# An attention and feed-forward kernel on one core: the activation h·erf(softplus(h)) as Softplus, Erf and one product, in place of Exp, Ln, a Newton step and Gelu

## The chip, the cores and the metric

The kernel runs on 1 core of one Trainium2 chip. The metric is device time in microseconds of one execution, as the median of several. One profiled execution of each kernel gives a trace; its span is from the first to the last instruction.

Engines in the profile: PE is TensorE's matmul, PEld its weight load, DVE is VectorE, ACT is ScalarE, POOL is GpSimd. The trace also gives the clock that TensorE was granted, as a share of full speed; below, "warm" is a stretch at 1.00 and "cold" one at 0.50, the two levels that single stretches show here.

## The reference, cut to what matters

```python
def _attn_ref(r, k, v, w, u):            # B, H, S, D = 4, 8, 768, 48
    for t in range(S):
        cur = einsum('bhd,bhe->bhde', u * kt, vt)
        y[:, :, t] = einsum('bhd,bhde->bhe', rt, state + cur)
        state = wt[..., None] * state + einsum('bhd,bhe->bhde', kt, vt)

def _moe_ref(x, w_in, w_out):            # x 3072 x 384, w_in 384 x 2048, w_out 2048 x 384
    h = x @ w_in
    sp = np.maximum(h, 0.0) + np.log1p(np.exp(-np.abs(h)))
    g = h * erf(sp)
    return g @ w_out
```

## The kernel before: the parts that matter

The attention works in 24 steps of 128 tokens; six steps (chunks) make one sequence. In a step, seven levels each do products `pp` of k and r on TensorE, then VectorE scales half of r and half of k in place (`in`), and the next level's products need them. Between the levels TensorE is given "fills": pieces of the feed-forward part, which works in units of two steps (256 tokens). TensorE's order is fixed by hand; the order on the other engines comes from a scheduler, and `in_turn` only keeps ScalarE's table passes in one sequence.

```python
for level in range(1, LOG + 1):
    ...                                   # pp = products of K and R (PE)
    fill(1)                               # one piece of feed-forward work (PE)
    for x, to, by in ((R, 1, 0), (K, 0, 1)):
        ...
        nc.vector.tensor_mul(half_of, half_of, tots[level - 1]...)        # "in"
    if level <= MASKED:
        nc.vector.copy_predicated(flat, mask..., pp...)                   # "a"
    else:
        ...  nc.scalar.copy(a[...], pp[...])
...                                       # y; transposes of K; the state's products
y_sb = ...; nc.scalar.copy(y_sb[:], y[:])
fill(1)
...                                       # transposes of y into xT

def hidden(xT, gs):                       # per group of 1024 columns; 4 groups to a unit
    in_turn(nc.scalar.preload_act_table_set("natural_log_exp_and_others"))
    ...                                   # h = x w_in (PE), copied by ACT
    nc.vector.tensor_scalar(out=ex[:], in0=h[:], scalar1=30.0, scalar2=None, op0=ALU.min)
    in_turn(nc.scalar.activation(ex[:], ex[:], AF.Exp, bias=e_bias[:]))
    in_turn(nc.scalar.activation(sp[:], ex[:], AF.Ln, bias=1.0, scale=1.0 / E_SCALE))
    in_turn(nc.scalar.activation(rc[:], sp[:], AF.Ln, bias=tiny[:]))
    in_turn(nc.scalar.activation(rc[:], rc[:], AF.Exp, scale=-1.0))
    nc.gpsimd.tensor_mul(er[:], sp[:], rc[:])
    nc.vector.scalar_tensor_tensor(out=rc[:], in0=er[:], scalar=2.0, in1=rc[:], ...)
    ...                                   # after the last group of the unit:
    in_turn(nc.scalar.activation(sp[:], sp[:], AF.Gelu, scale=math.sqrt(2.0)))

def gate(h, ex, sp, rc):
    nc.vector.scalar_tensor_tensor(out=low[:], in0=ex[:], ..., in1=ex[:], ...)
    nc.gpsimd.tensor_mul(rc[:], sp[:], rc[:])
    nc.vector.scalar_tensor_tensor(out=ex[:], in0=rc[:], ..., in1=ex[:], ...)
    nc.vector.scalar_tensor_tensor(out=ex[:], in0=low[:], ..., in1=ex[:], ...)
    nc.gpsimd.tensor_mul(h[:], ex[:], h[:])
```

The weights come as 64-bit numbers and are converted to fp32 at the start, by seven VectorE and two GpSimd passes per tile (24 tiles of w_in, 16 of w_out).

Of the kernel before, what the change touches and what calls it, by code (L numbers as in the profile page):

```python
# [17 lines left out]
P = 128  # partitions, and the tokens of one chunk  # L18
EP = 64  # partitions from one head of a pair to the other
UNIT = 256  # tokens of one feed-forward unit  # L20
GC = 1024  # columns of one group of the activation

# The decays between two tokens s < t of one chunk are split where the blocks of
# 2, 4, .. 128 tokens that hold both have their middle: at its level each pair
# gets (product of w from the middle up to t-1) x (product of w from s+1 up to
# the middle), so only products of w appear, never a quotient or a logarithm.
LOG = 7
MASKED = 5  # levels 1 .. MASKED are picked out of a full product by a mask


def rows(ap, n):
    """ap's last axis in rows of n"""
    return ap.rearrange("p (a b) -> p a b", b=n)
# [3 lines left out]
def kernel(  # L37
    ctx: ExitStack,
    tc: tile.TileContext,
    rkw: bass.AP,  # [step, e, d, (r k w), pair, t]  # L40
    v: bass.AP,  # [token, (h d)]
    u: bass.AP,  # [e, d, pair]
    w_in: bass.AP,
    w_out: bass.AP,
    masks: bass.AP,  # [s, level, t]
# [20 lines left out]
    act = ctx.enter_context(tc.tile_pool(name="act", bufs=NT // FG))  # L66
# [7 lines left out]
    # ---- what stays  # L74
# [8 lines left out]
    e_bias = const.tile([P, 1], FP32, name="e_bias")  # L83
    tiny = const.tile([P, 1], FP32, name="tiny")

    # The rows between the heads of a pair stay zero.
# [7 lines left out]
    E_SCALE = math.sqrt(2.0 / math.pi)  # L94
    LOW = math.sqrt(math.pi / 8.0)
    nc.vector.memset(e_bias[:], math.log(E_SCALE))
    nc.vector.memset(tiny[:], 1e-18)
# [11 lines left out]
    def load_weight(dst, src):  # L109
        """src into dst: fp32 as it is; fp64, of which the words come, rounded to fp32"""  # L110
        if src.dtype == FP32:
            nc.sync.dma_start(out=dst, in_=src)
            return
        n, f = dst.shape[1:]
        shape = [P, n, f]
        words = wide.tile([P, n, f, 2], I32, name="words")
        nc.sync.dma_start(
            out=words[:].rearrange("p n f two -> p n (f two)"), in_=src.bitcast(I32)
        )
        low, high = words[:, :, :, 0], words[:, :, :, 1]  # L120
        bits = wide.tile(shape, I32, name="bits")
        keep = wide.tile(shape, I32, name="keep")
        part = wide.tile(shape, FP32, name="part")
        SIGN, REST = -(1 << 31), (1 << 31) - 1
        # the exponent from 11 bits to 8, and the upper 20 bits of the mantissa
        nc.vector.tensor_scalar(
            out=bits[:], in0=high, scalar1=3, scalar2=1 << 30,
            op0=ALU.logical_shift_left, op1=ALU.bitwise_xor,
        )
        # what is below fp32's range is 0  # L130
        nc.vector.tensor_scalar(
            out=keep[:], in0=high, scalar1=REST, scalar2=None, op0=ALU.bitwise_and
        )
        nc.vector.tensor_scalar(
            out=keep[:], in0=keep[:], scalar1=float(0x382 << 20), scalar2=-1.0,
            op0=ALU.is_ge, op1=ALU.mult,
        )
        nc.vector.scalar_tensor_tensor(
            out=bits[:], in0=bits[:], scalar=REST, in1=keep[:],
            op0=ALU.bitwise_and, op1=ALU.bitwise_and,  # L140
        )
        nc.vector.scalar_tensor_tensor(
            out=bits[:], in0=high, scalar=SIGN, in1=bits[:],
            op0=ALU.bitwise_and, op1=ALU.bitwise_or,
        )
        # the lower 32 bits of the mantissa, by the power of two
        nc.vector.tensor_scalar(  # L147
            out=keep[:], in0=bits[:], scalar1=-(1 << 23), scalar2=None, op0=ALU.bitwise_and
        )
        nc.vector.tensor_scalar(  # L150
            out=part[:], in0=low.bitcast(U32), scalar1=2.0**-52, scalar2=None, op0=ALU.mult
        )
        nc.gpsimd.tensor_mul(part[:], part[:], keep[:].bitcast(FP32))  # L153
        nc.gpsimd.tensor_add(dst, part[:], bits[:].bitcast(FP32))
# [17 lines left out]
    def attend(s, xT, at, fill):  # L172
        """The tokens of step s, into the columns `at` of xT; fill(n) gives the tensor engine
        n pieces of other work."""
# [4 lines left out]
        # a[s, e, pair, t]: what v at s counts for in y at t  # L179
# [3 lines left out]
        def product(k, s0=0, t0=0, n=C, bank=None):  # L183
            """k of the n tokens from s0 on times R of those from t0 on"""
# [13 lines left out]
        # tots: the products of w over the blocks of 2**level tokens  # L198
# [11 lines left out]
        # A token with itself: through u.  # L210
# [9 lines left out]
        for level in range(1, LOG + 1):  # L220
# [8 lines left out]
            # R of the right halves by w of the left ones, K of the left by the right  # L229
# [20 lines left out]
        # y: from the chunks before, through the state, and from this one  # L250
# [23 lines left out]
        # the state behind this chunk, with zeros from head to head  # L274
# [36 lines left out]
    def in_turn(ins):  # L311
        """The activations in the order that switches tables least."""
        if last[0] is not None:
            tc.add_manual_dep(
                ins.ins,
                last[0].ins.name,
                mybir.DependencyInfo(mybir.DependencyClass.NoSync, mybir.DependencyReason.DATA),
                reason="activation tables",
            )
        last[0] = ins  # L320

    def hidden(xT, gs):
        """What gate() makes g / sqrt 2 of in h's place, g = h erf(sp), sp = log(1 + exp(h)),
        from gelu(z) = z (1 + erf(z / sqrt 2)) / 2 with z = sqrt(2) sp: erf(sp) / sqrt 2 =
        gelu(z) / sp - 1 / sqrt 2. Rounding would leave little of that far below h = 0: it is
        held between its bounds ex and ex - LOW ex^2, ex = sqrt(2 / pi) exp(h). Beyond h = 30
        erf(sp) is 1."""
        in_turn(nc.scalar.preload_act_table_set("natural_log_exp_and_others"))
        groups = []
        for g in range(NT // FG):  # L330
            h = hid.tile([P, FG, UNIT], FP32, name="h")
            for j in range(FG // 2):
# [14 lines left out]
            ex = act.tile([P, FG, UNIT], FP32, name="ex")  # L347
            sp = act.tile([P, FG, UNIT], FP32, name="sp")
            rc = act.tile([P, FG, UNIT], FP32, name="rc")
            nc.vector.tensor_scalar(  # L350
                out=ex[:], in0=h[:], scalar1=30.0, scalar2=None, op0=ALU.min
            )
            # ex = sqrt(2 / pi) exp(h)
            in_turn(nc.scalar.activation(ex[:], ex[:], AF.Exp, bias=e_bias[:]))  # L354
            in_turn(nc.scalar.activation(sp[:], ex[:], AF.Ln, bias=1.0, scale=1.0 / E_SCALE))  # L355
            # rc = 1 / sp, by a logarithm and a step of Newton
            in_turn(nc.scalar.activation(rc[:], sp[:], AF.Ln, bias=tiny[:]))  # L357
            in_turn(nc.scalar.activation(rc[:], rc[:], AF.Exp, scale=-1.0))  # L358
            er = act.tile([P, FG, UNIT], FP32, name="er", bufs=1)
            nc.gpsimd.tensor_mul(er[:], sp[:], rc[:])  # L360
            nc.vector.scalar_tensor_tensor(  # L361
                out=rc[:], in0=er[:], scalar=2.0, in1=rc[:],
                op0=ALU.subtract, op1=ALU.mult, reverse0=True,
            )
            groups.append((h, ex, sp, rc))
            if g == NT // FG - 1:
                for _, _, sp, _ in groups:
                    in_turn(nc.scalar.activation(sp[:], sp[:], AF.Gelu, scale=math.sqrt(2.0)))
                gs.extend(groups)
            yield  # L370

    def gate(h, ex, sp, rc):
        low = act.tile([P, FG, UNIT], FP32, name="low", bufs=1)
        nc.vector.scalar_tensor_tensor(  # L374
            out=low[:], in0=ex[:], scalar=-1.0 / LOW, in1=ex[:], op0=ALU.add, op1=ALU.mult
        )
        nc.gpsimd.tensor_mul(rc[:], sp[:], rc[:])  # L377
        nc.vector.scalar_tensor_tensor(  # L378
            out=ex[:], in0=rc[:], scalar=-math.sqrt(0.5), in1=ex[:], op0=ALU.add, op1=ALU.min
        )  # L380
        nc.vector.scalar_tensor_tensor(  # L381
            out=ex[:], in0=low[:], scalar=-LOW, in1=ex[:], op0=ALU.mult, op1=ALU.max
        )
        nc.gpsimd.tensor_mul(h[:], ex[:], h[:])  # L384

    def project(i, gs):
        """out of unit i"""
        for t in range(SPU):
# [12 lines left out]
            nc.scalar.mul(out=o[:], in_=ps[:], mul=math.sqrt(2.0))  # L401
# [3 lines left out]
    def pieces():  # L405
        """The feed-forward work in pieces of six or four products: half of a unit's hidden
        layer, half of the projection of the unit before, and again."""
# [47 lines left out]
def level_masks():  # L455
    """[s, level, t]: whether s and t meet at that level"""
# [45 lines left out]
```

## Time and profile before

| | before |
|---|---|
| median of 4 runs | 1239.9 us (1238.8 to 1246.9) |
| span of the profiled execution | 1249.1 us |
| start to step 2; step 2; step 3 | 114.3; 78.2; 53.0 us |
| steps 4 to 23 | 905.3 us |
| after the attention (tail) | 98.3 us |

The stages are read from the timeline of TensorE: each step begins with the products of `uk`. The page's first part gives each engine's busy time, with its share of the span and its instructions:

```profile
PE 959.8 (77%) x6232; PEld 725.6 (58%) x6232; DVE 877.3 (70%) x1040; ACT 413.3 (33%) x524; POOL 638.4 (51%) x438
```

### The profile page before, as it was taken

The page shows a single profiled execution, that of the slowest core. Times are in us where ns is not written, and L with a number is a line of the kernel's source. Part 1 is how long each engine was busy: PE and PEld are TensorE (multiplying, and loading weights), DVE is VectorE, ACT ScalarE, POOL GpSimd, SP SyncE. Part 2 cuts the span into 40 slices and gives each one's busy share as a digit, 9 for nine tenths or more (in the row PEclk, how much of TensorE's full clock was granted, in tenths as well). Part 3 has the DMA queues.
Part 4 walks back from the last instruction along what each step waited for, and adds up shares of the span by engine and source line. Part 5 has one row for each costly group of instructions (what it writes and reads, how often), then busy time and mean ns, then how long its engine had stood idle before and what let it go on. Part 6 is the DMA issues. An engine that isn't in the chain of part 4 may idle for free.

```text
span 1249.1 us, 15339 instructions
## 1 busy us (share of the span) xinstructions
PE 959.8 (77%) x6232; PEld 725.6 (58%) x6232; DVE 877.3 (70%) x1040; ACT 413.3 (33%) x524; POOL 638.4 (51%) x438
## 2 busy tenths in 40 slices
PE   3336528489699798798898898898898898898847
PEld 2336426467466666666666666666675675675624
DVE  6898884774875945946966936937957837838563
ACT  0001113333345136145135226225244324324440
POOL 5756562831933923923825725715627527516362
PEclk9999657599799689789798888888897887888978
DMA  5323211101100100100110110110010010000000
GB/s 137 93 80 107 73 53 26 26 1 33 32 19 15 32 20 13 32 20 13 33 32 1 33 33 1 32 33 18 15 33 20 14 33 7 1 7 7 7 6 13
DMA packets 16086, 37.49 MB, mean 30 GB/s; under 512 B 2320, under 2 KB 8464, under 8 KB 16016
## 3 DMA queue, kind: packets, MB, share of 16 engines
q1 hardware_dynamic: 16016, 36.51, 11.3%
q8 instruction: 49, 0.80, 0.3%
q14 instruction: 21, 0.17, 0.1%
HBM read 31.79 MB, written 4.72 MB: 29 GB/s over the span
## 4 chain that ended last, share of the span: by engine, by line
DVE 41%; PE 22%; ACT 13%; issue 11%; POOL 10%; DMA 1%; POOLq 0%; SPq 0%; DVEq 0%; ACTq 0%
DVE ex L378 8%; DVE in L234 7%; POOL er L360 7%; PE m L391 6%; PE m L337 6%; DVE low L374 6%; DVE ex L381 6%; PE pp L189 4%; ACT ex L354 3%; ACT rc L357 3%; ACT sp L355 3%; ACT rc L358 3%; DVE a L240 2%; DVE ex L350 2%; POOL part L153 2%
## 5 line engine op out<-in xcount | busy, mean ns | idle before, releaser
L391 PE MATMUL m<-w_out_sb,h 128*128 128x384 f32 x768 | 298.0, 538 | 25.4 <-POOL h L384 20.0
L360 POOL TENSOR_TENSOR er<-sp,rc 128x1024 f32<-128x1024 f32 x48 | 113.2, 2357 | 385.3 <-ACT rc L358 385.3
L189 PE MATMUL pp<-in 48*128 48x128 f32 (+2 forms) x3072 | 192.1, 275 | 144.3 <-DVE in L234 144.3
L337 PE MATMUL m<-xT,w_in_sb 128*128 128x256 f32 x1152 | 300.4, 416 | 0.6 <-ACT xT L307 0.6
L189 PEld LDWEIGHTS pp<-in 48*128 48x128 f32 (+2 forms) x3072 | 164.7, 181 | 199.8 <-issue 195.9
L337 PEld LDWEIGHTS m<-xT,w_in_sb 128*128 128x128 f32 x1152 | 231.4, 207 | 46.2 <-issue 3.1
L391 PEld LDWEIGHTS m<-w_out_sb,h 128*128 128x128 f32 x768 | 153.9, 210 | 125.8 <-POOL h L384 28.7
L234 DVE TENSOR_TENSOR in<-in,tot_sb 128x256 f32<-128x256 f32 x284 | 154.5, 579 | 47.5 <-PE pp L189 47.5
L361 DVE SCALAR_TENSOR_TENSOR rc<-er,rc 128x1024 f32<-128x1024 f32 x48 | 84.1, 1752 | 142.0 <-POOL er L360 142.0
L384 POOL TENSOR_TENSOR h<-ex,h 128x1024 f32<-128x1024 f32 x48 | 133.3, 2777 | 47.1 <-DVE ex L381 47.1
L344 ACT COPY h<-m 128x512 f32<-128x512 f32 x96 | 55.7, 580 | 306.4 <-PE m L337 306.4
L240 DVE COPY_PREDICATED a<-mask_sb,pp 128x1024 f32<-128x1024 int32 x120 | 155.9, 1299 | 0.0
L377 POOL TENSOR_TENSOR rc<-sp,rc 128x1024 f32<-128x1024 f32 x48 | 145.1, 3044 | 0.2
L378 DVE SCALAR_TENSOR_TENSOR ex<-rc,ex 128x1024 f32<-128x1024 f32 x48 | 103.5, 2156 | 6.8 <-POOL rc L377 3.9
L255 PE MATMUL y<-s,in 128*128 128x96 f32 x160 | 50.1, 409 | 66.3 <-DVE in L234 66.3
L374 DVE SCALAR_TENSOR_TENSOR low<-ex 128x1024 f32<-128x1024 f32 x48 | 95.2, 1983 | 2.3 <-ACT ex L354 1.2
L153 POOL TENSOR_TENSOR part<-part,keep 128x256 f32<-128x256 f32 (+1 forms) x40 | 61.6, 1540 | 56.9 <-DVE keep L147 56.9
L354 ACT ACTIVATE ex<-ex,e_bias 128x1024 f32<-128x1024 f32 x48 | 55.2, 1149 | 103.7 <-DVE ex L350 101.1
L207 POOL TENSOR_TENSOR tot_sb<-tot_sb 128x128 f32<-128x128 f32 (+5 forms) x140 | 79.9, 571 | 9.2
L265 PE MATMUL y<-v_sb,a 128*128 128x48 f32 x384 | 78.4, 349 | 6.5 <-ACT a L248 6.5
L255 PEld LDWEIGHTS y<-s,in 128*128 128x128 f32 x160 | 36.7, 282 | 77.3 <-DVE in L234 77.3
L265 PEld LDWEIGHTS y<-v_sb,a 128*128 128x128 f32 x384 | 76.7, 281 | 7.8 <-ACT a L248 7.0
(50 smaller groups left out, 943.9 us busy)
## 6 DMA issues: line engine op xcount, KB each, us to landing
in<-in_rkw SPq DMA_DIRECT2D x48, 288.0 KB, 4.6
words<-in_moe_w_in SPq DMA_DIRECT2D x24, 256.0 KB, 2.7
words<-in_moe_w_out SPq DMA_DIRECT2D x16, 384.0 KB, 3.1
v_sb<-in_v SPq DMA_DIRECT2D x24, 192.0 KB, 2.5
out<-o SPq DMA_DIRECT2D x24, 192.0 KB, 1.9
mask_sb<-in_masks SPq DMA_DIRECT2D x1, 320.0 KB, 3.4
u_sb<-in_u SPq DMA_DIRECT2D x2, 0.8 KB, 2.0
```

The lines of the kernel that those rows point to most:

```text
L189: nc.tensor.matmul(pp[s0 : s0 + n, e, p, t0 : t0 + n], lhsT=k[at_, p, s0 : s0 + n], rhs=R[at_, p, t0 : t0 + n], start=True, stop=True,)
L234: nc.vector.tensor_mul(half_of, half_of, tots[level - 1][:, :, by : by + 1].to_broadcast([P, nb, half]),)
L240: nc.vector.copy_predicated(flat, mask_sb[:, level - 1 : level, :].to_broadcast([P, NE * NP, C]), pp[:].rearrange("p e n t -> p (e n) t"),)
L265: nc.tensor.matmul(y[:, h], lhsT=a[:, e, p, :], rhs=vt[:, h], start=not c, stop=True, skip_group_check=True,)
L337: nc.tensor.matmul(ps[:, q, :], lhsT=w_in_sb[:, kk, f * P : (f + 1) * P], rhs=xT[:, kk, :], start=kk == 0, stop=kk == KT - 1,)
L354: in_turn(nc.scalar.activation(ex[:], ex[:], AF.Exp, bias=e_bias[:]))
L360: nc.gpsimd.tensor_mul(er[:], sp[:], rc[:])
L374: nc.vector.scalar_tensor_tensor(out=low[:], in0=ex[:], scalar=-1.0 / LOW, in1=ex[:], op0=ALU.add, op1=ALU.mult)
L377: nc.gpsimd.tensor_mul(rc[:], sp[:], rc[:])
L378: nc.vector.scalar_tensor_tensor(out=ex[:], in0=rc[:], scalar=-math.sqrt(0.5), in1=ex[:], op0=ALU.add, op1=ALU.min)
L384: nc.gpsimd.tensor_mul(h[:], ex[:], h[:])
L391: nc.tensor.matmul(ps[:], lhsT=gs[f // FG][0][:, f % FG, t * P : (t + 1) * P], rhs=w_out_sb[:, f, :], start=f == 0, stop=f == NT - 1,)
```

## The change

The intent: ScalarE has Softplus and Erf as functions of its own, so the activation needs two table passes and one product, and the roundabout through Exp, Ln, a Newton step, Gelu and a clamp goes. The diff, cut to its core (comments, which also went, left out):

```diff
-    act = ctx.enter_context(tc.tile_pool(name="act", bufs=NT // FG))
+    act = ctx.enter_context(tc.tile_pool(name="act", bufs=2 * NT // FG))
...
-        in_turn(nc.scalar.preload_act_table_set("natural_log_exp_and_others"))
+        in_turn(nc.scalar.preload_act_table_set("softplus"))
...
-            ...                     # min, Exp, Ln, Ln, Exp, er, rc as above
+            in_turn(nc.scalar.activation(sp[:], h[:], AF.Softplus))
...
-                    in_turn(nc.scalar.activation(sp[:], sp[:], AF.Gelu, scale=math.sqrt(2.0)))
+                    in_turn(nc.scalar.activation(sp[:], sp[:], AF.Erf))
...
-    def gate(h, ex, sp, rc):
-        ...                         # low, rc, ex, ex, h as above
+    def gate(h, sp):
+        nc.vector.tensor_mul(h[:], h[:], sp[:])
...
-            nc.scalar.mul(out=o[:], in_=ps[:], mul=math.sqrt(2.0))
+            nc.scalar.copy(o[:], ps[:])
```

More of the change, by code (lines that the diff above doesn't have):

```diff
@@ L1 @@
-import math
 from contextlib import ExitStack
@@ L82 @@
     w_out_sb = const.tile([P, NT, DM], FP32, name="w_out_sb")
-    e_bias = const.tile([P, 1], FP32, name="e_bias")
-    tiny = const.tile([P, 1], FP32, name="tiny")
     nc.vector.memset(in_bufs[0][:], 0.0)
@@ L93 @@
     make_identity(nc, ident[:])
-    E_SCALE = math.sqrt(2.0 / math.pi)
-    LOW = math.sqrt(math.pi / 8.0)
-    nc.vector.memset(e_bias[:], math.log(E_SCALE))
-    nc.vector.memset(tiny[:], 1e-18)
     loaded = {}
@@ L346, in hidden @@
                     yield
-            ex = act.tile([P, FG, UNIT], FP32, name="ex")
             sp = act.tile([P, FG, UNIT], FP32, name="sp")
-            rc = act.tile([P, FG, UNIT], FP32, name="rc")
-            nc.vector.tensor_scalar(
-                out=ex[:], in0=h[:], scalar1=30.0, scalar2=None, op0=ALU.min
-            )
-            in_turn(nc.scalar.activation(ex[:], ex[:], AF.Exp, bias=e_bias[:]))
-            in_turn(nc.scalar.activation(sp[:], ex[:], AF.Ln, bias=1.0, scale=1.0 / E_SCALE))
-            in_turn(nc.scalar.activation(rc[:], sp[:], AF.Ln, bias=tiny[:]))
-            in_turn(nc.scalar.activation(rc[:], rc[:], AF.Exp, scale=-1.0))
-            er = act.tile([P, FG, UNIT], FP32, name="er", bufs=1)
-            nc.gpsimd.tensor_mul(er[:], sp[:], rc[:])
-            nc.vector.scalar_tensor_tensor(
-                out=rc[:], in0=er[:], scalar=2.0, in1=rc[:],
-                op0=ALU.subtract, op1=ALU.mult, reverse0=True,
-            )
-            groups.append((h, ex, sp, rc))
+            in_turn(nc.scalar.activation(sp[:], h[:], AF.Softplus))
+            groups.append((h, sp))
             if g == NT // FG - 1:
-                for _, _, sp, _ in groups:
-                    in_turn(nc.scalar.activation(sp[:], sp[:], AF.Gelu, scale=math.sqrt(2.0)))
+                for _, sp in groups:
+                    in_turn(nc.scalar.activation(sp[:], sp[:], AF.Erf))
                 gs.extend(groups)
             yield
-    def gate(h, ex, sp, rc):
-        low = act.tile([P, FG, UNIT], FP32, name="low", bufs=1)
-        nc.vector.scalar_tensor_tensor(
-            out=low[:], in0=ex[:], scalar=-1.0 / LOW, in1=ex[:], op0=ALU.add, op1=ALU.mult
-        )
-        nc.gpsimd.tensor_mul(rc[:], sp[:], rc[:])
-        nc.vector.scalar_tensor_tensor(
-            out=ex[:], in0=rc[:], scalar=-math.sqrt(0.5), in1=ex[:], op0=ALU.add, op1=ALU.min
-        )
-        nc.vector.scalar_tensor_tensor(
-            out=ex[:], in0=low[:], scalar=-LOW, in1=ex[:], op0=ALU.mult, op1=ALU.max
-        )
-        nc.gpsimd.tensor_mul(h[:], ex[:], h[:])
+    def gate(h, sp):
+        nc.vector.tensor_mul(h[:], h[:], sp[:])
     def project(i, gs):
```

## The prediction

> **What bounds the kernel now.** I read the page's busy shares and chain first, then the list of waits, then the timeline of one step, and last the stretch table. On the page TensorE (PE) is busy 77% and VectorE (DVE) 70% of the span, so no engine is plainly full. The chain of work that ended last is mostly VectorE:
>
> ```profile
> DVE 41%; PE 22%; ACT 13%; issue 11%; POOL 10%; DMA 1%; POOLq 0%; SPq 0%; DVEq 0%; ACTq 0%
> ...
> L374 DVE SCALAR_TENSOR_TENSOR low<-ex 128x1024 f32<-128x1024 f32 x48 | 95.2, 1983 | 2.3 <-ACT ex L354 1.2
> ```
>
> The list of waits (total us, times, longest) says what TensorE is held up by:
>
> ```profile
> PE pp L189 <- DVE in L234: 144.3, 41, 11.3
> ...
> PE y L255 <- DVE in L234: 66.3, 20, 5.5
> ```
>
> Both are the same thing: the attention scales its r and k in place on VectorE (`in`) between two levels, and the next products wait. These scalings are short; what makes them late is seen in the timeline (start, us, engine, idle before) of the last part of one step:
>
> ```profile
> 757.72 1.16 PE L189 MATMUL pp<-in 48*128 48x128 f32 x16
> 758.81 2.85 PE L391 MATMUL m<-w_out_sb,h 128*128 128x384 f32 x8
> 761.59 0.60 PE L189 MATMUL pp<-in 48*32 48x32 f32 x32
> 762.12 2.85 PE L391 MATMUL m<-w_out_sb,h 128*128 128x384 f32 x8
> 764.90 0.68 PE L189 MATMUL pp<-in 48*64 48x64 f32 x16
> 765.51 2.85 PE L391 MATMUL m<-w_out_sb,h 128*128 128x384 f32 x8
> 767.66 5.64 POOL L377 TENSOR_TENSOR rc<-sp,rc 128x1024 f32<-128x1024 f32 x2
> 767.69 3.42 DVE L361 SCALAR_TENSOR_TENSOR rc<-er,rc 128x1024 f32<-128x1024 f32 x1 [4.53 <-POOL er L360]
> 771.03 2.89 DVE L234 TENSOR_TENSOR in<-in,tot_sb 128x256 f32<-128x256 f32 x2
> 773.64 0.74 PE L255 MATMUL y<-s,in 128*128 128x96 f32 x2 [5.28 <-DVE in L234]
> 774.18 0.98 PE L265 MATMUL y<-v_sb,a 128*128 128x48 f32 x4
> ```
>
> Up to 768.3 TensorE has no gap. Then `in` stands in VectorE's queue behind `rc` (L361), which had waited 4.53 us for GpSimd's (POOL's) `er`, and both then run against GpSimd: 2.89 us for two scalings that take 0.75 us elsewhere in the step. TensorE stands for 5.28 us and is slower afterwards. So the activation reaches the critical path through VectorE's queue, GpSimd's latency and contention between these two, not through TensorE's own work. The stretch table, from the start of step 4 to the end of the attention (length; then busy time and count of PE, PEld, DVE, ACT, POOL; clock), gives the size:
>
> ```profile
> 245.50:1150.80 905.30, 775.28 (x5189) 582.36 (x5188) 629.89 (x627) 344.00 (x437) 445.49 (x275) 0.87 0.08 20
> ```
>
> Twenty steps take 905.3 us, 45.3 each; TensorE idles 130 us of it (6.5 a step), at a clock of 0.87.
>
> **What the Trainium skill says.** (1) "ScalarE: Activation LUTs", What ACT_TABLE_LOAD costs: every function has the same per-element cost, and a switch of table costs the same for every set (1283 ns for the load). The trace agrees: Gelu 1045 ns and Ln, Exp 1057 ns (1149 ns with a bias tile), 24 loads of 1283 ns. So I give Softplus and Erf 1.05 us each. (2) "VectorE: DVE Perf Modes", The TRN2 errata: an fp32 tensor_tensor takes (N+151)/0.96 ns, 1.22 us for 1024; the trace's `a` (L214) took 1.223 us. (3) "GPSIMD Engine Reference", Specifications: GpSimd's SBUF interfaces are shared with VectorE, and two-input VectorE instructions contend. The trace agrees: L374 takes 1.199 us at its least, 3.265 at its most. (4) "TensorE: Matmul & The Clock Gate", Part 1: after an idle window of some 3.4 us the clock halves. The trace agrees: sixteen `pp` records take 1.16 us in a dense stretch and 2.08 us after the 4.12 us wait at 702.8.
>
> **The change part by part,** per group of 1024 columns (48 groups):
> - VectorE loses five passes: means of 802 + 1752 + 1983 + 2156 + 1644 ns = 8.34 us, 400 us in all. It gains one product of 1.22 us, 59 us. Its busy time goes from 877 to about 535 us, and to some 510 if the contention goes with it.
> - GpSimd loses `er`, `rc` and `h`: 2357 + 3044 + 2777 ns = 8.18 us, 392 us in all, and keeps about 247 us. Two hand-overs from VectorE to GpSimd and back vanish.
> - ScalarE loses five passes, 258 us by the rows, and gains two, 48 x 2 x 1.05 = 101 us: 413 to about 255 us. The number of table loads stays at 24 in the order of instructions. sqrt(2) in the output copy was free and stays so.
> - TensorE's instructions and their order do not change, nor does a byte from or to HBM.
>
> So the question is how short a step is when TensorE never waits. I add it up from warm stretches of the timeline. From `uk` at 741.31 to the last fill's end at 768.28 there is no gap: 26.97. The y products take 2.71 warm (730.38 to 733.09), the transposes of k with the wait for their copy 1.74, the state's products 1.81, the last fill 2.79 warm, and the transposes of y 0.42: **36.4 us**. The last chunk of a sequence has no state part (-3.55): 32.9 us. Of the 20 steps 4 are such, and 3 are a first chunk (about 1 us less each): 16 x 36.4 + 4 x 32.9 - 3 = 711 us, against 905: **-194 us**. Some 130 of this are waits; the rest is the clock.
>
> Does the rest of the new work fit under 36.4? VectorE has per step 14 scalings (5.3), five masked copies (6.5), 1.23 and 0.72 for `a` and the state, and two products on average (2.4): 16 us. ScalarE about 11 us. One place is tight: in the second step of each unit, softplus of the last group, the table load and four Erf follow the fourth fill, and the order of instructions has two products ahead of the level-6 scalings. From the fourth fill's end: copy to +0.7, softplus +1.75, load +3.1, Erf done at +4.1 and +5.0, products done at +6.5, scalings +7.25, which the next `pp` wants at +7.2. I allow 0.3 us a unit, 3 us in all.
>
> The first 114 us load and convert the weights, with no activation in them: unchanged. Step 2 (114.3 to 192.5) still converts 13 tiles of w_out. About 6 us of the activation's VectorE passes and its waits on GpSimd go: an estimate of 78 to 67. Step 3 (53.0) becomes a dense step with a cold start, 40. Together **-24**. The tail (1150.8 to 1249.1, 98.3 us) holds 24 pieces of fill at 2.79 = 67 us plus 3.5 us from the last product to the end; the last unit's softplus, load, Erf and product (8.4 us) lie under the last four pieces of the projection before it (11.1 us). So 70.5, **-28**.
>
> Sum: 1249.1 - 194 + 3 - 24 - 28 = 1006 us of profiled span. The timed median is 0.992 of it (1239.2 to 1249.1): 998. For waits that I do not see I add 1%: **1010 us**.
>
> **Rivals.** (a) *VectorE stays the limit of each level*, its queue held by the product that waits for Erf. For it: instructions are in order, and two products stand ahead of scalings. If each unit lost 3 us so, and the clock fell each time, 12 units would cost 40 to 60 us: 1050 to 1070. Against it: the sums above. (b) *ScalarE becomes the blocker*: the load and four Erf stand ahead of the copies of `a` that y needs. For it: y waited for them twice before, 6.5 us in all. Against it: the slack is about 1 us and ScalarE has less to do than before. A few us a unit: again about 1050. (c) *The gain is nearly nothing because the activation was hidden.* Then the waits for `in` would remain; but they begin behind the removed instructions in the timeline. I give it little. (d) The conversion in step 2 is bound by VectorE and GpSimd anyway and nothing is won there: +11 us.
>
> **Range and chances.** Without any new wait about 995, with (a) or (b) in every unit 1060; I take 980 to 1055. A gain under 2% would need nearly all waits to come back: faster 0.97, same 0.02, slower 0.01.
>
> **What would show it.** Right: TensorE busy above 90% between step 4 and the end of the attention at a clock near 1, steps of 36 to 38 us, waits for `in` under 30 us in total, VectorE near 520 us, GpSimd near 240, scalings at 0.41 us, a tail near 71 us. Wrong: TensorE still waiting for `in` with h<-h,sp just ahead of it (a), y waiting for the copy of `a` (b), Softplus costing more than 1.1 us, or step 2 still at 78 us (d).

## The result, and the profile after

The changed kernel takes 974.9 us in the median of 4 runs (973.4 to 980.0) and is correct. The ratio to the kernel before is 0.785, with a 95% interval of 0.781 to 0.789. A ratio here is not quite the ratio of the medians quoted. The prediction had the direction, the size within 4% and the mechanism, but 974.9 lies below its range of 980 to 1055: its pieces of TensorE work were sized too long, above all in the dense step.

| stage, us of span | before | predicted | after |
|---|---|---|---|
| start to step 2 | 114.3 | 114.3 | 112.6 |
| step 2 | 78.2 | 67 | 66.6 |
| step 3 | 53.0 | 40 | 37.4 |
| steps 4 to 23 | 905.3 | 714 | 688.3 |
| tail | 98.3 | 70.5 | 66.6 |
| sum | 1249.1 | 1006 | 971.6 |

The page of the changed kernel, busy times and the chain that ended last:

```profile
PE 852.1 (88%) x6232; PEld 649.6 (67%) x6232; DVE 485.2 (50%) x846; ACT 258.3 (27%) x380; POOL 191.1 (20%) x294
...
PE 80%; DVE 11%; POOL 3%; ACT 3%; issue 2%; DMA 1%; SPq 0%; POOLq 0%; ACTq 0%; DVEq 0%
```

The chain now runs through TensorE. TensorE itself is busy 108 us less with the same 6232 instructions, at a mean granted clock of 0.965 in place of 0.862. The waits of TensorE for the scalings (total us, times, longest):

```profile
PE pp L182 <- DVE in L227: 72.3, 19, 7.8
...
PE y L248 <- DVE in L227: 6.9, 3, 4.3
```

Of 210.6 us 79.2 are left, and they lie in the first four steps: between 250 and 900 us the list of waits has none of them. (Before, 92 of the 210.6 lay in the first four steps too.) The stretch table from step 4 to the end of the attention (length; busy time and count of PE, PEld, DVE, ACT, POOL; clock) shows TensorE standing 11.9 us of 688.3, at full clock:

```profile
216.67:905.00 688.33, 676.43 (x5189) 510.23 (x5188) 308.19 (x468) 214.08 (x316) 67.97 (x154) 1.00 0.11 26
```

So of the 217 us that these twenty steps lost, 118 were waits of TensorE (130 to 12) and 99 were the same products done at a higher clock (775.3 to 676.4, the clock from 0.87 to 1.00). In the tail TensorE had waited another 25.5 us for the last unit's own activation (20.0 for `h` of the gate, 5.5 for ScalarE's copy), which the list no longer has. The timeline of the end of a step, the place that the prediction showed with a stop of 5.28 us:

```profile
616.03 3.90 ACT L342 ACTIVATE sp<-sp 128x1024 f32<-128x1024 f32 x4
616.81 0.60 PE L182 MATMUL pp<-in 48*32 48x32 f32 x32
617.12 2.36 DVE L347 TENSOR_TENSOR h<-h,sp 128x1024 f32<-128x1024 f32 x2 [0.96 <-ACT sp L342]
617.34 2.85 PE L354 MATMUL m<-w_out_sb,h 128*128 128x384 f32 x8
619.39 0.76 DVE L227 TENSOR_TENSOR in<-in,tot_sb 128x256 f32<-128x256 f32 x2
620.07 2.35 DVE L347 TENSOR_TENSOR h<-h,sp 128x1024 f32<-128x1024 f32 x2
620.29 0.68 PE L182 MATMUL pp<-in 48*64 48x64 f32 x16
620.91 2.85 PE L354 MATMUL m<-w_out_sb,h 128*128 128x384 f32 x8
622.34 0.76 DVE L227 TENSOR_TENSOR in<-in,tot_sb 128x256 f32<-128x256 f32 x2
623.59 0.36 PE L248 MATMUL y<-s,in 128*128 128x96 f32 x2
```

Two products of the gate do stand in VectorE's queue ahead of the scalings, as the prediction's rival (a) has it, but each pair takes 2.36 us with GpSimd at rest, and y begins on time.

### The profile page after: what moved, and what is told of

Read it like the earlier page. It is cut to its first block, busy times and chain, and to the rows that moved or that the text cites. A ratio compares the mean times of both kernels' runs of the same rounds, so it can differ in the third digit from the quotient of the medians. Undisturbed runs are those within 1.5% of the kernel's fastest.

```text
span 971.6 us, 14797 instructions
## 1 busy us (share of the span) xinstructions
PE 852.1 (88%) x6232; PEld 649.6 (67%) x6232; DVE 485.2 (50%) x846; ACT 258.3 (27%) x380; POOL 191.1 (20%) x294
## 4 chain that ended last, share of the span: by engine, by line
PE 80%; DVE 11%; POOL 3%; ACT 3%; issue 2%; DMA 1%; SPq 0%; POOLq 0%; ACTq 0%; DVEq 0%
PE m L354 27%; PE m L327 26%; PE pp L182 17%; PE y L258 4%; PE tr L276 2%; PE y L248 2%; POOL part L146 2%; DVE keep L124 2%; DVE bits L119 1%; DVE part L143 1%; DVE keep L127 1%; DVE bits L135 1%; DVE bits L131 1%; ACT kT L273 1%; DVE keep L140 1%
## 5 line engine op out<-in xcount | busy, mean ns | idle before, releaser
L327 PE MATMUL m<-xT,w_in_sb 128*128 128x256 f32 x1152 | 279.7, 394 | 0.6 <-ACT xT L300 0.6
L354 PE MATMUL m<-w_out_sb,h 128*128 128x384 f32 x768 | 268.1, 495 | 0.0
L327 PEld LDWEIGHTS m<-xT,w_in_sb 128*128 128x128 f32 x1152 | 216.7, 194 | 39.3 <-issue 0.9
L227 DVE TENSOR_TENSOR in<-in,tot_sb 128x256 f32<-128x256 f32 x284 | 109.9, 423 | 193.5 <-PE pp L182 193.5
L347 DVE TENSOR_TENSOR h<-h,sp 128x1024 f32<-128x1024 f32 x48 | 56.9, 1229 | 52.7 <-ACT sp L342 52.7
L207 DVE TENSOR_TENSOR a<-pp,ident 128x1024 f32<-128x1024 f32 x24 | 29.4, 1225 | 90.8 <-PE pp L182 90.7
L241 ACT COPY a<-pp 32x256 f32<-32x256 f32 (+1 forms) x72 | 31.1, 432 | 153.3 <-DVE a L233 82.0
L338 ACT ACTIVATE sp<-h 128x1024 f32<-128x1024 f32 x48 | 50.7, 1057 | 1.5
L342 ACT ACTIVATE sp<-sp 128x1024 f32<-128x1024 f32 x48 | 46.8, 1045 | 0.1
L248 PE MATMUL y<-s,in 128*128 128x96 f32 x160 | 36.4, 313 | 6.9 <-DVE in L227 6.9
L200 POOL TENSOR_TENSOR tot_sb<-tot_sb 128x128 f32<-128x128 f32 (+5 forms) x140 | 40.2, 287 | 10.4
L182 PE MATMUL pp<-in,uk 48*128 48x128 f32 x384 | 32.5, 316 | 10.3 <-POOL uk L205 10.3
```

What stands on the lines that cost most here:

```text
L182: nc.tensor.matmul(pp[s0 : s0 + n, e, p, t0 : t0 + n], lhsT=k[at_, p, s0 : s0 + n], rhs=R[at_, p, t0 : t0 + n], start=True, stop=True,)
L200: nc.gpsimd.tensor_mul(tot, pair[:, :, 0], pair[:, :, 1])
L227: nc.vector.tensor_mul(half_of, half_of, tots[level - 1][:, :, by : by + 1].to_broadcast([P, nb, half]),)
L248: nc.tensor.matmul(y[:, p * W2 : (p + 1) * W2], lhsT=R[:, p, :], rhs=S[:, p, :], start=True, stop=False, skip_group_check=True,)
L327: nc.tensor.matmul(ps[:, q, :], lhsT=w_in_sb[:, kk, f * P : (f + 1) * P], rhs=xT[:, kk, :], start=kk == 0, stop=kk == KT - 1,)
L338: in_turn(nc.scalar.activation(sp[:], h[:], AF.Softplus))
```

## The experiments

Thirteen further kernels ran, all correct. The theory: the activation cost its time through VectorE's queue and through contention with GpSimd, and TensorE's clock fell after the waits. Rivals: ScalarE's passes; the sheer amount of VectorE work; GpSimd alone; no clock effect.

| label | what it is | median us | ratio to before (95%) |
|---|---|---|---|
| e1_act | changed + 3 ScalarE passes per group | 986.0 | 0.793 (0.788 to 0.797) |
| e2_pool | changed + 3 GpSimd products per group | 1092.6 | 0.878 (0.873 to 0.883) |
| e3_dve | changed + 4 VectorE passes per group | 1016.5 | 0.817 (0.812 to 0.822) |
| e4_both | both of these, unconnected | 1200.2 | 0.964 (0.959 to 0.969) |
| e5_chain | both, as one chain between the engines | 1227.7 | 0.987 (0.981 to 0.992) |
| e6_before_nopool | before, its 3 GpSimd products on VectorE | 1173.4 | 0.943 (0.939 to 0.948) |
| e8_wait | changed + a wait before y | 1250.3 | 1.006 (1.001 to 1.012) |
| e9_wait_fill | the same + 8 useless products in the wait | 1250.0 | 1.005 (1.000 to 1.010) |
| e9b_wait_fill12 | the same with 12 | 1200.4 | 0.966 (0.963 to 0.970) |
| e9c_fill_where_wait | 12, only where there is a wait | 1184.2 | 0.954 (0.948 to 0.959) |
| e10_late | changed, w_out converted in steps 2 and 3 | 958.6 | 0.772 (0.769 to 0.774) |
| e11_conv_dve | changed, conversion without GpSimd | 994.2 | 0.800 (0.798 to 0.803) |
| e12_conv_late | both of these | 952.4 | 0.766 (0.764 to 0.769) |

### What was taken away, put back piece by piece (e1 to e5)

The extra passes write a tile that nobody reads. Those of e2 to e5 read h after the gate's product and are left out for the last unit, so no result is made from them; what they do is occupy an engine, and hold h's buffer longer (ScalarE's copy into h waited for that three times in e4, 13 us in all).

```diff
 # e1_act, behind Softplus
+            for _ in range(3):
+                ja = junk.tile([P, FG, UNIT], FP32, name="ja")
+                in_turn(nc.scalar.activation(ja[:], h[:], AF.Softplus))
 # e2_pool, in gate, behind the product
+        for _ in range(3):
+            jp = junk.tile([P, FG, UNIT], FP32, name="jp")
+            nc.gpsimd.tensor_mul(jp[:], h[:], h[:])
 # e3_dve, in the same place (e4_both has both loops)
+        for _ in range(4):
+            jd = junk.tile([P, FG, UNIT], FP32, name="jd")
+            nc.vector.tensor_mul(jd[:], h[:], h[:])
```

> The changed kernel with three further Softplus passes per group of 1024 columns on ScalarE, into a tile that nobody reads: 48 x 3 x 1.06 = 152 us more of ScalarE, which is then as busy (some 410 us) as in the kernel before. My theory (the time was lost in VectorE's queue): at most 1% over the changed kernel's 975 us, so 975 to 985. Rival (the three ScalarE passes that went are what was saved): a good part of the 265 us comes back, over 1050 us.

> The changed kernel with three products per group on GpSimd, which read the finished h and write a tile that nobody reads: GpSimd at some 580 us as before, no hand-over to VectorE. My theory: contention lengthens the scalings, but VectorE has room, so 980 to 1015 us, with more of the wait of the products for the scalings and a clock a little under 1. Rival (GpSimd's occupation and contention alone made the loss): over 1100 us.

> The changed kernel with four further passes of 128x1024 per group on VectorE (48 x 4 x 1.22 = 234 us, so VectorE some 720 us), with no GpSimd in them. My theory: the scheduler puts one or two passes between two scalings and a level has 3.9 us for 2 us of its own work, so little is lost: 975 to 1010 us. Rival (the sheer amount of VectorE work was the bound): over 1100 us.

> Both at once and unconnected: four VectorE passes and three GpSimd products per group. My theory: contention stretches the passes ahead of the scalings to 2 us and more, so waits and half clock come back in part: 1010 to 1100 us, clearly over the sum of the two single costs. Rival (the costs just add): the sum of what the two single runs lose, within 10 us.

Measured: e1 986.0, 11 us over the changed kernel; that is 1 us more than expected, and far from the rival. ScalarE as busy as before (402 us) costs next to nothing; what it costs shows as 12 waits of y for the copy of `a`, 11.2 us in all, which is the prediction's rival (b) in small. e3 1016.5, 42 us, a little over the range of 975 to 1010. e2 1092.6, 118 us: the expectation of 980 to 1015 missed badly, and the rival's "over 1100" is nearly reached, though GpSimd was busy only 466 us and not the expected 580. The timeline of e2 says why:

```profile
682.20 12.53 POOL L353 TENSOR_TENSOR jp<-h 128x1024 f32<-128x1024 f32 x5 [19.60 <-DVE h L348]
683.17 4.14 DVE L228 TENSOR_TENSOR in<-in,tot_sb 128x256 f32<-128x256 f32 x2
...
687.46 1.12 PE L183 MATMUL pp<-in 48*64 48x64 f32 x16 [3.50 <-DVE in L228]
```

GpSimd works off five products in a row. The two scalings beside it take 4.14 us instead of the 0.76 of the lines further up, about as long as two of these GpSimd products (2.12 us each in the mean of e2), and TensorE stops for 3.50 us although VectorE's queue held nothing more than in the changed kernel. So contention with GpSimd did more here than stretch VectorE's passes by some share of their length: a scaling of 0.38 us that met these products took about as long as one of them. I had taken it for a stretching and thought that VectorE's slack would hide it.

e4 took 1200.2, 225 us over the changed kernel and clearly over the sum of 42 and 118: together they cost some 66 us more. It was expected to be super-additive, though the range of 1010 to 1100 was too low by the same misjudged contention.

The fifth puts the same seven passes into one chain that goes to and fro, as the old activation did:

```diff
+        nc.gpsimd.tensor_mul(one[:], h[:], h[:])
+        nc.vector.tensor_mul(two[:], one[:], h[:])
+        nc.gpsimd.tensor_mul(one[:], two[:], h[:])
+        for _ in range(3):
+            nc.vector.tensor_mul(two[:], one[:], h[:])
+        nc.gpsimd.tensor_mul(one[:], two[:], h[:])
```

> The same four VectorE passes and three GpSimd products as in the run with both, but as one chain that goes to and fro between the two engines (GpSimd, VectorE, GpSimd, three on VectorE, GpSimd), as the activation before did. If the hand-overs in VectorE's queue cost something beside contention, it is slower than the 1200 us of the unconnected pair, near the 1240 of before: 1210 to 1280. If contention between the two engines is all, the chain keeps them apart (each waits for the other) and it is faster than 1200: 1080 to 1180.

It took 1227.7 us, within the range for "hand-overs cost something beside contention" and 27.5 us over e4 with the same number of passes. The same seven passes, with no numerics in them, bring back 253 of the 265 us between the two kernels. They do so by another mixture: TensorE waits 254.8 us for the scalings (210.6 before) but is busy only 923.7 us (959.8 before, 852.1 changed), so more of it is waits and less is clock, and that the totals come so close may in part be luck. The extra passes also sit behind the gate in a bunch, not where the old ones were. The parts do not add up simply, so no exact share of the 265 belongs to any one; what is shown is that passes on VectorE and GpSimd alone are enough to bring nearly all of it back, and that ScalarE's passes by themselves bring 11 us. No run has ScalarE inside the chain, as the old activation had it.

### The kernel before without GpSimd in its activation (e6)

```diff
-            nc.gpsimd.tensor_mul(er[:], sp[:], rc[:])
+            nc.vector.tensor_mul(er[:], sp[:], rc[:])
```

and the same for `rc` and `h` in gate.

> The kernel before with its three products of the activation on VectorE in place of GpSimd: eight passes per group on VectorE, none on GpSimd, arithmetic the same. Theory contention: the scalings fall from 0.58 to about 0.43 us on average and the time falls well under before in spite of three passes more on VectorE: 1030 to 1120 us. Rival (VectorE's amount of work is the bound): it has about as many busy microseconds as before, so no gain: 1220 us or more.

It took 1173.4 us: 5.7% under before, and between the two ranges. Contention is nearly gone, as expected: the scalings read (columns: busy us, mean ns | idle before)

```profile
L234 DVE TENSOR_TENSOR in<-in,tot_sb 128x256 f32<-128x256 f32 x284 | 113.6, 427 | 65.7 <-PE pp L189 65.7
```

against 154.5 us and 579 ns before. But VectorE is as busy as before (854.8 to 877.3 us) with eight passes a group, and TensorE still waits 182 us for the scalings. So both theories hold a part: handing products to a slower engine beside VectorE lost 68 us against doing them on VectorE itself, and most of the 265 needs the passes to be gone altogether.

### The clock, by itself (e8, e9)

```diff
 # e8_wait, at each step from 2 on: R is unchanged by it
+            if level == LOG and s >= SPU:
+                for _ in range(14):
+                    nc.vector.scalar_tensor_tensor(
+                        out=R, in0=R, scalar=1.0, in1=R, op0=ALU.mult, op1=ALU.max)
 # e9_wait_fill: also, before the products of y (which overwrite it)
+            for _ in range(8):
+                nc.tensor.matmul(y[:], lhsT=ident[:], rhs=w_out_sb[:, 0, :],
+                                 start=True, stop=True, skip_group_check=True)
```

> The changed kernel with fourteen in-place passes over r (times 1, max with itself: the result is unchanged) ahead of the last level's scaling, so that TensorE waits some 6.5 us before y in the 19 steps from step 2 on that are not a first chunk. If the clock halves after such a wait, a step with state gains the wait and about 4.3 us more (y 2.6 to 5.2, transposes of k and the wait 1.3 to 1.7, state products 1.0 to 1.8, fill 2.6 to about 3.5): 975 + 19 x 6.5 + 19 x 4 = some 1175 us, 1140 to 1210. Without a clock effect only the waits: about 1100.

> The same waits, but TensorE does eight useless products of 128x384 into the bank of y during the wait (16 records, about 5.2 us, overwritten by y). If the clock is what makes the products after the wait slow, they stay warm: y 2.6 us, state products 1.0, and about 4 us a step less than the run with the wait alone, so some 75 us less although TensorE does more: 1085 to 1125 us. If the clock has nothing to do with it, the same time as with the wait alone.

e8 took 1250.3, over its range. The fourteen passes depend on each other and took 0.72 us each, so the wait was 8.1 us and not 6.5. The list of waits has 185.6 us for y against 6.9 in the changed kernel, 179 us more; the time went up by 275. The remaining 97 us are, but for 4.5 us more of waits for the scalings at `pp`, not waits. A step shows them:

```profile
742.88 0.74 PE L253 MATMUL y<-s,in 128*128 128x96 f32 x2 [8.13 <-DVE in L232]
...
748.04 1.08 PE L276 MATMUL tr<-ident,in 128*128 128x128 f32 x4
749.79 2.02 PE L281 MATMUL tr<-v_sb,kT 128*128 128x96 f32 x8 [0.68 <-ACT kT L278]
751.61 4.16 PE L359 MATMUL m<-w_out_sb,h 128*128 128x384 f32 x8
755.61 0.49 PE L304 MATMUL tr<-ident,y_sb 128*128 128x128 f32 x3
```

The trace's own record of the granted clock agrees: it falls from 1.00 to 0.50 inside the wait, at about 737.3, and comes back at about 754.4, in the fill.

e9 showed no gain (1250.0), and I take it for a failed experiment rather than an answer. Sized for a shorter wait, its eight products ended 3 to 4.3 us before y in the steps looked at; at 748.1 y began warm (0.46 us for its first two records) and fell to 0.71 within it, at 797.3 it was cold from the start. It also did its products in the three first-chunk steps that have no wait. So two more:

> The wait before y again, now with twelve useless products (24 records, some 7.8 us) in it, because the eight of the run before ended 3 us before y and the clock had time to fall. In the run with the wait alone a step took 48.3 us: 34.8 of the changed kernel, 8.1 of wait, so 5.4 of slower products. If the half clock is the cause, y takes 2.6 us again, the state products about 1.0, and some 5 us a step come back in 15 to 19 steps: 1150 to 1180 us. If the products after the wait are slow for another reason (the y products wait for something else), no change: 1245 to 1255.

> The run with twelve useless products once more, without them in the three first-chunk steps that have no wait: there they were pure cost (41.6 us a step against 33.9), which I had not meant. If the half clock explains all of what the wait costs beyond itself: 1200 - 3 x 7.8 = 1177 us, 1170 to 1185, so some 73 us under the run with the wait alone, in which TensorE does less. Any other reason: no nearer to that than 1195.

e9b took 1200.4 us, over its range of 1150 to 1180, and e9c, without the products where there is no wait, 1184.2 us, just inside its range: 66 us less than with the same wait left idle, though TensorE does more work. Its step reads

```profile
705.17 7.90 PE L253 MATMUL y<-w_out_sb,ident 128*128 128x384 f32 x24
713.47 0.46 PE L259 MATMUL y<-s,in 128*128 128x96 f32 x2 [0.39 <-DVE in L232]
...
716.18 0.62 PE L282 MATMUL tr<-ident,in 128*128 128x128 f32 x4
717.47 1.13 PE L287 MATMUL tr<-v_sb,kT 128*128 128x96 f32 x8 [0.68 <-ACT kT L284]
718.44 2.77 PE L365 MATMUL m<-w_out_sb,h 128*128 128x384 f32 x8
721.05 0.49 PE L310 MATMUL tr<-ident,y_sb 128*128 128x128 f32 x3
```

From y to the transposes of y it is 7.58 us here and 12.73 us in e8 (first y product to the first transpose of y), for the same instructions, and here the granted clock stays at 1.00 throughout. That the products after a long wait are slow because of the clock is thereby shown. Of the 97 us the filling gave back 66; in some steps (49.0 to 49.2 us against 43.2) it did not bridge the whole wait, and the clock fell again.

### Two versions meant to be better (e10 to e12)

What is left beside full TensorE steps is the start: 216.7 us to step 4, with VectorE's queue full of weight conversion.

```diff
 # e10_late
-    for i in range(NT):
-        load_w_out(i)
+    late = {(s, k): 8 * s + k - 16 for s in (2, 3) for k in range(8)}
...                                     # in fill(), the k-th call of step s:
+                if (s, k) in late:
+                    load_w_out(late[s, k])
 # e11_conv_dve (e12_conv_late has both)
-        nc.gpsimd.tensor_mul(part[:], part[:], keep[:].bitcast(FP32))
-        nc.gpsimd.tensor_add(dst, part[:], bits[:].bitcast(FP32))
+        nc.vector.tensor_mul(part[:], part[:], keep[:].bitcast(FP32))
+        nc.vector.tensor_add(dst, part[:], bits[:].bitcast(FP32))
```

> A version meant to be better: the changed kernel with the sixteen loads and conversions of w_out called one by one at the levels of steps 2 and 3, not all before step 0. Theory: step 2 (66.6 us) is long because VectorE's queue holds conversions ahead of the scalings; spread out, 955 to 968 us. Rival: VectorE and GpSimd are the bound of the conversion however it is ordered, and step 4 waits for w_out instead: 970 to 980 us.

> The changed kernel with the two GpSimd passes of the weight conversion on VectorE. Theory contention: single-source VectorE passes that take 1.15 us beside GpSimd take 0.35 us, so the first 179 us shrink although VectorE does more: 940 to 962 us. Rival (VectorE's amount of work bounds the start): 33 us more of VectorE passes and no gain: 975 to 1005 us.

> Both of these: conversion on VectorE alone, and w_out's spread over steps 2 and 3. If each takes away part of the same queue: 935 to 958 us, the best of the versions. If one of them is all: the same as the better of the two within 5 us.

e10 took 958.6, within its range: step 4 begins at 201.6 us instead of 216.7. e11 took 994.2, in the rival's range, but not for the rival's reason. VectorE's single-source conversion passes did become short (`keep` of w_out from 763 to 354 ns), yet with GpSimd out of the way the order on VectorE put nearly all of w_out's conversion ahead of one scaling of step 1:

```profile
140.49 2.08 PE L182 MATMUL pp<-in 48*128 48x128 f32 x16 [50.73 <-DVE in L227]
```

e12, with that order mended, took 952.4 us, within its range, 22.5 us under the changed kernel and the best of all; its interval does not touch that of the changed kernel. It beats both kernels.

## Why the prediction was wrong, point by point

- **What bounds the kernel before**: right as far as the runs go. The activation reached the end through VectorE's queue, GpSimd and the clock: e5 brings 253 of 265 us back with passes on those engines alone, e1 11 with ScalarE.
- **Costs of the parts**: Softplus 1057 and Erf 1045 ns and 24 loads of 1283 ns, as said; the gate's product 1.229 us against 1.22 (the formula that the prediction cites is the page's for an add; the `a` that it checked it on reads PSUM, the gate's product does not). VectorE 485 us busy against "some 510", GpSimd 191 against 247: GpSimd's own small products also became shorter (the `tot_sb` products from 571 to 287 ns), which the sum had left out.
- **The step that failed: the dense step of 36.4 us.** "I add it up from warm stretches" was not true for two of its terms. The transposes of k with their wait (1.74) and the state's products (1.81) were read at 733.09 to 736.64, where the granted clock was 0.50. The step that was read; a step of the same kernel that begins a sequence and has no wait before y; and the place of the first after the change:

```profile
733.09 1.06 PE L278 MATMUL tr<-ident,in 128*128 128x128 f32 x4
734.83 2.02 PE L283 MATMUL tr<-v_sb,kT 128*128 128x96 f32 x8 [0.68 <-ACT kT L280]
736.64 4.41 PE L391 MATMUL m<-w_out_sb,h 128*128 128x384 f32 x8
```

```profile
643.10 0.62 PE L278 MATMUL tr<-ident,in 128*128 128x128 f32 x4
644.39 1.13 PE L283 MATMUL tr<-v_sb,kT 128*128 128x96 f32 x8 [0.68 <-ACT kT L280]
645.36 2.77 PE L391 MATMUL m<-w_out_sb,h 128*128 128x384 f32 x8
```

```profile
660.99 0.62 PE L271 MATMUL tr<-ident,in 128*128 128x128 f32 x4
662.28 1.13 PE L276 MATMUL tr<-v_sb,kT 128*128 128x96 f32 x8 [0.67 <-ACT kT L273]
663.25 2.77 PE L354 MATMUL m<-w_out_sb,h 128*128 128x384 f32 x8
665.86 0.49 PE L299 MATMUL tr<-ident,y_sb 128*128 128x128 f32 x3
```

  From start to start, the transposes with their wait are 1.29 us instead of 1.74, the state's products 0.97 instead of 1.81, the fill 2.61 instead of 2.79, y 2.61 instead of 2.71, and the stretch of the levels 26.88 instead of 26.97. That is 34.8 us a step, 1.66 less, and 16 such steps make 26.6 us; the two cold terms are 1.29 of the 1.66, 21 us in all. The fill's 2.79 was no cold reading: it is the distance between starts for a fill between two levels, and the last fill of a step is followed sooner. The clock's part was 99 us where "the rest is the clock" had left 64. e8 and e9c show the same two sets of durations at will.

  The trace of the kernel before had the warm numbers: in 4 of its 16 steps with a state part from step 4 on, three of which begin a sequence, the transposes took 0.62 us and the state's products 1.13. And the wait need not be long. In the step that was read TensorE had stood only 1.09 us (729.3 to 730.4), with no other gap in the 18 us before; y still ran warm, and the clock fell at 733.1. All six steps with a wait of 1.09 us before y from step 4 on went so, which "after an idle window of some 3.4 us" did not lead one to expect; in the changed kernel, without that wait, the same products of y leave the clock at 1.00.
- **Start and tail**: step 2 was 66.6 against 67, step 3 37.4 against 40, the first two steps 1.7 shorter. The tail was 66.6 against 70.5: its 24 pieces follow each other without the attention's products, and (66.6 - 3.5) / 24 is 2.63 us a piece where 2.79 was used. With the 25.7 us of steps 4 to 23 (714 to 688.3) these make the 34 us by which the sum of spans was too long.
- **The two corrections at the end** were a second, smaller mistake, and they nearly cancel. "The timed median is 0.992 of it" took a scatter for a rule: time is span plus some 1.8 us, and the profiled run before was one of its slower ones (seven runs of before in the rounds of e5: 1239.2 to 1242.1 five times, 1249.8 and 1251.1). That took 8 us off wrongly. The 1% for "waits that I do not see" added 12 us; there are none in the dense steps. Without both, 1006 of span would have been about 1008 of time.
- **Rivals**: (a) in every unit the products of the gate stand ahead of the scalings, but a second step of a unit takes only 0.2 us more than a first (34.97 to 34.78 us). (b) no more than 1.3 us. (c) fell. (d) fell: step 2 shrank as said.
- **Signs named**: TensorE at 98% and the clock at 1.00 fit; waits for the scalings under 30 us in total did not (79.2 us), since the start has them as before, though from 250 us on there are none. Steps of 36 to 38 us did not fit: 34.8 to 35.0.

Left open: why 10 of the 32 runs of before took 1245.7 to 1251.1 us and the other 22 took 1238.0 to 1242.3, and how the 265 us divide between VectorE's queue, contention and the clock, which act on each other.

## What to carry to other kernels

A dense step must be summed from pieces that ran at full clock: check each term's duration, and the granted clock beside it, against a stretch with no wait ahead of it, above all when the wait that one removes nearly always stands before those very pieces. Here three steps of the old trace lacked the wait and had the right numbers. A small, in-order instruction on the critical path is made late by what stands ahead of it in its engine's queue, and a scaling on VectorE also by GpSimd working beside it, so work on "idle" GpSimd is not free for VectorE: three products per group that no one waited for cost 118 us. Waits of TensorE cost more than their length (some 5 us more per 8 us here), so removing them gains more than the idle time shows.

## What the Trainium skill lacked or had wrong

- "TensorE: Matmul & The Clock Gate", Part 4, says that the full clock does not engage for transposes. Here four fp32 transposes of 128x128 took 0.62 us in a stretch at a granted clock of 1.00 and 1.08 us at 0.50, so inside other work they follow the clock. Whether transposes by themselves would bring the clock up, which the page's reason is about, no run here shows.
- The same page, Part 1, says that some 3.4 us of sustained activity bring the full clock back. In the run with the wait the clock came back only some 11.5 us after TensorE had resumed (742.9 to 754.4): 6.2 us of products of y and transposes without a gap, a gap of 0.68 us and the state's products all ran at 0.50, and only the fill after them sped up. The state's products were cold (2.02 us) behind every such wait from step 4 on. What share of activity counts as busy is not told, and no run here settles it.
- No page that I read has the effect of useless products in a wait: 66 us gained in the run with twelve of them, and nothing with eight that ended 3 us or more too early.
